# A pre-norm layer with a long convolution and a token mixer: the last inverse shuffles all on GpSimd's queue, the shortcut past them taken out, and the order of every engine written anew

## The chip, the cores and the metric

The kernel runs on one core of a Trainium2 chip. The metric is the device time of one execution in microseconds (us), lower is better. A core has five engines that run side by side, each through a queue of its own, in order: TensorE (PE; its weight loads are shown apart as PEld), VectorE (DVE), ScalarE (ACT), GpSimd (POOL) and SyncE (SP), which here only issues transfers. Transfers (DMAs) are issued by SP, POOL and once by ACT, and run on 16 DMA engines.

## The reference

```python
x = A_q                                            # 1 x 2048 x 448 (B, S, D), bf16
kv = k_shift * v          # k_shift: causal 4-tap filter of A_k along S, taps A_shift_k per channel
y  = irfft(rfft(kv, 2S) * rfft(ssm_k, 2S))[:S]     # per channel, a causal convolution of length 2048
h  = x + layernorm(x) * (y + kv * ssm_D)
u  = layernorm(layernorm(h))                       # over D
u  = gelu(einsum("bsd,sf->bdf", u, w1) + b1)       # mixes along S; F = 1792
out = h + (einsum("bdf,fs->bds", u, w2) + b2).transpose(0, 2, 1)
```

## The kernel before

The sequence index is s = 16 q + r: q is the partition (128), r a row (0 to 15) of 448 channels. The convolution is a discrete Fourier transform in two stages of matmuls, of the filter ("k", from `A_ssm_k`) and of kv ("u"), a product, and an inverse in two stages. All of SBUF is one tensor, `arena`; all of PSUM is `ps`, eight banks that are handed out to matmul groups and come free when a group is copied out (an "eviction", on ACT or DVE).

The steps, by the names that the order of work uses:

- `dummy`, `tables`, `loads`: matmuls on a constant (fillers, L1001), the sine tables E and the block matrices, and the loads. SP issues the loads of k, of the filter's four chunks of channels (L863; three of 128 rows, one of 64 rows of 4 KB) and of v.
- `kv`: transposes of k (L942), the 4-tap filter as small matmuls (L968), times v on DVE (L983).
- `kT`: transposes of the filter (L1014), eight for each half of a chunk, evicted to `KT`; behind the second half of each of the first three chunks three fillers (`N_WK`).
- `k1`, `u1` (`emit_stage1`, matmuls L1035): first stage. 16 groups each; an eviction (L1045) and, for each two groups, three shuffles (L1051) that move data to other partitions: two of 112 KB from POOL's queue, one of 224 KB from SP's. `k2`, `u2` (`emit_stage2`, L1070): second stage, evictions L715/L718 for k and L714/L717 for u, into `TK` and `TU`. One eviction covers 128 x 896.
- `i1` (`emit_products_i1`): DVE multiplies (L1136, 128 x 1792) each of 16 columns of TU with TK; for each pair of columns jj = 0 to 7, 16 matmuls (L1153), two evictions (L714, back into TU), and the inverse shuffles to `TZ` (L1176): for each of the two columns, one of 112 source rows (196 KB) on POOL's queue and one of 16 source rows (28 KB) on SP's. The small ones carry rows r = 14 and 15. In the order's names, the matmuls of jj sit in the steps i1.1, i1.4, i1.6, i1.8, i1.10, i1.12, i1.14 and i1.16; operations 9 and 18 (in i1.4 8 and 17) are the evictions, the next four the shuffles, so i1.10:19 and i1.10:21 are POOL's two.
- `ct`: transposes E into `ET` (L1084).
- `i2` (`emit_i2`): for each row r two matmuls of ET with TZ (L1275), then the gate, h, and the norms: for r below 4 an operation on DVE (L1312), for the others a gate on ACT or DVE (L1292, L1294) and L1302 on DVE; statistics on ACT, DVE and POOL; and the normalised row into `Q` (L1361, DVE).
- `mlp`: seven groups accumulate over the 16 rows of Q (L1408, seven matmuls a row, seven of the eight banks); seven more groups (L1418); then the second matrix, 16 rows of 14 matmuls (L1430), an addition on DVE (L1433) and the stores.

**The shortcut.** The last pair, jj = 7, is special before the change. Its block matrices are a permuted copy (`ML`, made on POOL in `emit_ew`), its evicted columns stay in TU, and its shuffles are four transfers of 98 KB for the rows r = 2 to 15, on SP's queue and ACT's (L1165). For r = 0 and 1 (`NZ` = 2) the data of jj = 7 are not waited for: the places are filled with zeros by two transfers, four small ones gather the needed parts of ET into `EW`, and four more matmuls for each of these two rows (L1283) add the contribution straight from TU.

**What sets the order.** `ORDER` holds, for each engine, the sequence of all its operations, found beforehand by a search. `schedule()` runs through these queues with a model of durations to hand out PSUM banks and other ring buffers; it then emits the instructions, each with the waits on semaphores that its operands need. An engine waits at the head of its queue. POOL's DMAs share eight semaphores in turn, so the ninth waits until the first has landed. The four loads of the first matrix's first half are `w1a.0` to `w1a.3` (L1381); the last three wait for the last inverse shuffles (`shuf["zl"]`).

Of the kernel before, what the change touches and what calls it, by code (L numbers as in the profile page):

```python
# [13 lines left out]
        "dummy.0:1-9 kv.4:0-11 kv.3:0-7 kv.6:0-11 kv.5:0-7 kT.1:0-7 kT.0:0-3 kT.1:9-11 kT.0:4-7 kT.3:0-7 kT.2:0-3 "  # L14
        "kT.3:9-11 kT.5:0-7 kT.2:4-7 kT.5:9-10 kT.6:0-7 kT.7:0-7 bias.0:0 kT.5:11 kv.7:0-7 k1.8:0-7 k1.9:0-7 "
        "k1.12:0-7 k1.10:0-7 kv.1:0-7 kv.2:0-11 k1.11:0-7 k1.15:0-7 k1.14:0-7 k1.13:0-7 kT.4:0-7 kv.8:0-11 "
        "kv.12:0-23 kv.9:0-27 kv.10:0-23 kv.11:0-27 k1.4:0-7 k1.0:0-1 u1.0:0-7 k1.0:2-7 u1.1:0-7 u1.2:0-7 k1.1:0-7 "
        "u1.3:0-7 kv.13:0-27 u1.4:0-7 k1.5:0-7 kv.14:0-23 k1.6:0-7 u1.6:0-7 k1.2:0-7 u1.5:0-7 kv.15:0-27 k1.7:0-7 "
        "u1.7:0-7 u1.8:0-7 u1.9:0-7 k1.3:0-7 k2.0:0-3 k2.1:0-3 k2.12:0-3 k2.13:0-3 k2.4:0-3 k2.5:0-3 kv.16:0-23 "
        "k2.9:0-3 k2.8:0-3 u1.10:0-7 u1.12:0-7 u1.13:0-7 u1.14:0-7 u1.15:0-7 u1.11:0-7 k2.2:0-3 k2.3:0-3 k2.6:0-3 "  # L20
        "k2.7:0-3 k2.10:0-3 k2.11:0-3 k2.15:0-3 k2.14:0-3 u2.0:0-3 u2.1:0-3 u2.13:0-3 u2.12:0-3 u2.8:0-2 u2.9:0-3 "
        "u2.8:3 u2.7:0-3 u2.6:0-3 i1.1:1-7 i1.1:10-16 i1.1:8 i1.1:17 i1.14:10-16 i1.14:1-7 i1.14:17 i1.14:8 "
        "i1.8:1-7 i1.8:10-17 i1.8:8 ct0.0:0-7 u2.10:0-3 u2.11:0-3 i1.10:1 i1.10:10-17 i1.10:2-8 u2.4:0-3 u2.5:0-3 "
        "i1.12:1-8 i1.12:10-17 u2.3:0-3 u2.2:0-3 i1.6:1-8 i1.6:10-17 u2.15:0-3 u2.14:0-3 i1.4:9-15 i1.4:0-7 i1.4:16 "
        "i1.16:1-7 i1.16:10-17 i1.16:8 ct.1:0-7 ct.0:0-7 ct.2:0-7 warm.0:0 i2.1:0-1 i2.2:0-3 i2.9:0-1 i2.10:0-3 "
        "i2.17:0-1 i2.45:0-1 i2.32:0-1 i2.20:0-1 i2.54:0-1 i2.28:0-1 warm.1:0 i2.41:0-1 mlp.0:1 mlp.0:4 mlp.0:2 "
        "mlp.0:0 mlp.0:6 mlp.0:3 i2.58:0-1 mlp.0:5 mlp.1:6 mlp.1:5 mlp.1:4 mlp.1:1 mlp.1:0 mlp.1:3 mlp.1:2 "
        "i2.67:0-1 mlp.2:3 mlp.2:2 mlp.2:1 mlp.2:5-6 mlp.2:4 mlp.2:0 mlp.3:4-5 mlp.3:2 mlp.3:1 mlp.3:3 mlp.3:0 "
        "mlp.3:6 i2.71:0-1 mlp.4:4 mlp.4:2 mlp.4:1 mlp.4:5 mlp.4:3 mlp.4:6 mlp.4:0 i2.80:0-1 mlp.5:1-2 mlp.5:4 "
        "mlp.5:6 mlp.5:5 mlp.5:0 mlp.5:3 i2.84:0-1 mlp.6:0 mlp.6:6 mlp.6:1 mlp.6:5 mlp.6:2 mlp.6:4 mlp.6:3 "  # L30
        "i2.93:0-1 mlp.7:6 mlp.7:0-1 mlp.7:5 mlp.7:3-4 mlp.7:2 mlp.8:2 mlp.8:6 mlp.8:5 mlp.8:3-4 mlp.8:0-1 mlp.9:3 "
        "mlp.9:1 mlp.9:6 mlp.9:0 mlp.9:5 mlp.9:4 mlp.9:2 i2.97:0-1 mlp.10:3 mlp.10:0 mlp.10:2 mlp.10:4-6 mlp.10:1 "
        "mlp.11:0 mlp.11:3 mlp.11:2 mlp.11:5 mlp.11:4 mlp.11:6 mlp.11:1 mlp.12:4 mlp.12:1 mlp.12:3 mlp.12:5 "
        "mlp.12:0 mlp.12:6 mlp.12:2 mlp.13:5 mlp.13:2 mlp.13:0 mlp.13:6 mlp.13:3 mlp.13:1 mlp.13:4 mlp.14:3 "
        "mlp.14:0 mlp.14:2 mlp.14:1 mlp.14:5 mlp.14:4 mlp.14:6 mlp.15:5 mlp.15:1 mlp.15:6 mlp.15:0 mlp.15:3 "
        "mlp.15:2 mlp.15:4 mlp.17:0-15 mlp.18:0-15 mlp.19:0-15 mlp.20:0-15 mlp.21:0-15 mlp.22:0-15 mlp.23:0-15 "
        "mlp.24:0-13 mlp.25:0-13 mlp.26:0-13 mlp.27:0-13 mlp.28:0-13 mlp.29:0-13 mlp.30:0-13 mlp.31:0-13 "
        "mlp.32:0-13 mlp.33:0-13 mlp.34:0-13 mlp.35:0-13 mlp.36:0-13 mlp.37:0-13 mlp.38:0-13 mlp.39:0-10 "
        "mlp.39:16-17 mlp.39:11 mlp.39:18-20 mlp.39:12 mlp.39:21-22 mlp.39:13 mlp.39:23-29 "
    ),  # L40
    "act": (
        "tables.0:5 kv.4:12 kv.3:8 kv.6:12 tables.6:3 tables.5:3 tables.7:5 bias.0:1 k1.8:8 k1.9:8 k1.10:8 k1.11:8 "
        "k1.13:8 k1.14:8 k1.15:8 k1.4:8 u1.0:8 u1.1:8 u1.2:8 u1.4:8 k1.5:8 k1.6:8 u1.5:8 u1.6:8 k1.7:8 u1.8:8 "
        "u1.9:8 k2.1:4 k2.13:4-5 k2.5:5 k2.9:4 u1.12:8 u1.13:8 u1.14:8 u1.15:8 k2.3:5 k2.7:5 k2.11:4 k2.15:4 u2.1:4 "
        "u2.13:5 u2.13:4 u2.9:5 u2.9:4 u2.7:4-5 i1.1:9 i1.1:18 i1.14:9 i1.14:18 i1.8:18 i1.8:9 u2.11:4-5 i1.10:18 "
        "i1.10:9 u2.5:4 i1.12:9 i1.12:18 u2.3:5 u2.3:4 i1.6:9 i1.6:18 u2.15:4-5 i1.4:8 i1.4:17 xn.1:0 xn.2:0 "
        "i1.16:18 i1.16:9 i1.16:21 ct.0:8 ct.2:8 xn.5:0 xn.4:0 ct.1:8 i2.46:0 i2.33:0 i2.19:0 i2.29:0 i2.22:0 "
        "i2.42:0 i2.31:0 i2.59:0 i2.35:0 i2.44:0 i2.68:0 i2.48:0 i2.72:0 i2.57:0 i2.81:0 i2.61:0 i2.70:0 i2.74:0 "
        "i2.94:0 i2.83:0 i2.87:0 i2.96:0 i2.100:0 mlp.16:1-2 mlp.16:6 mlp.16:4 mlp.16:0 mlp.16:3 mlp.16:5 mlp.17:16 "
        "mlp.18:16 mlp.19:16 mlp.20:16 mlp.21:16 mlp.22:16 mlp.23:16 mlp.39:15 "  # L50
    ),
    "dve": (
        "dummy.0:0 tables.3:0-1 kv.0:3 tables.6:0 tables.4:16 tables.5:0 tables.4:17 tables.6:1 tables.4:18 "
        "tables.5:1 tables.4:19 tables.6:2 tables.4:20 tables.5:2 kT.1:8 tables.7:6 kT.0:8 kT.3:8 tables.7:4 "
        "tables.7:7 kv.5:8 kT.5:8 kT.2:8 kT.7:8 kT.6:8 bias.1:0 kv.7:8 k1.12:8 kv.1:8 kv.2:12 kv.0:4 kT.4:8 kv.8:12 "
        "kv.12:24-25 kv.9:28-29 kv.10:24-25 kv.11:28-29 k1.0:8 k1.1:8 u1.3:8 kv.13:28-29 kv.14:24-25 k1.2:8 "
        "kv.15:28-29 u1.7:8 k1.3:8 k2.1:5 k2.5:4 kv.16:24-25 k2.9:5 u1.10:8 u1.11:8 k2.3:4 k2.7:4 k2.11:5 k2.15:5 "
        "u2.1:5 i1.0:0 i1.1:0 i1.14:0 i1.13:0 i1.7:0 i1.8:0 i1.9:0 i1.10:0 ct0.0:8 q.1:2 q.1:0 i1.11:0 i1.12:0 "
        "q.1:1 q.1:3 u2.5:5 i1.5:0 q.2:0 i1.6:0 i1.3:0 i1.2:0 q.2:1-2 q.3:0 i1.15:0 xn.0:1 q.2:3 i1.16:0 q.3:2 "
        "q.3:1 q.3:3 q.5:0 q.5:2 q.5:1 q.4:2 q.5:3 q.7:0 q.4:0 q.4:3 q.4:1 q.7:2 xn.3:1 q.6:0 q.6:2 q.6:1 q.6:3 "  # L60
        "i2.3:0 i2.4:0 i2.11:0 i2.5:0 i2.18:0 i2.6:0 i2.12:0 i2.21:0 i2.13:0 i2.8:0 i2.14:0 i2.55:0 i2.30:0 i2.16:0 "
        "i2.34:0 i2.43:0 i2.26:0 q.7:3 q.7:1 i2.47:0 i2.27:0 q.8:2 q.8:0 q.8:3 q.8:1 i2.39:0 i2.56:0 i2.40:0 "
        "i2.73:0 i2.60:0 i2.69:0 i2.52:0 i2.82:0 i2.85:0 i2.53:0 i2.86:0 i2.65:0 i2.66:0 i2.78:0 i2.79:0 i2.95:0 "
        "i2.98:0 i2.99:0 i2.92:0 i2.91:0 i2.105:0 i2.104:0 mlp.24:14 mlp.25:14 mlp.26:14 mlp.27:14 mlp.28:14 "
        "mlp.29:14 mlp.30:14 mlp.31:14 mlp.32:14 mlp.33:14 mlp.34:14 mlp.35:14 mlp.36:14 mlp.37:14 mlp.38:14 "
        "mlp.39:14 mlp.39:30 "
    ),
# [109 lines left out]
class _Sched:  # L177
# [145 lines left out]
    def schedule(self):  # L323
# [235 lines left out]
def _build(nc, A_q, A_k, A_v, A_shift_k, A_ssm_k, A_ssm_D, B_w1, B_b1, B_w2, B_b2, out):  # L559
# [8 lines left out]
    R = 16  # L568
# [924 lines left out]
```

## Time and profile before

| what | us |
|---|---|
| runs (median) | 174.29, 175.18, 176.02 (175.18) |
| profiled execution | 173.93 |
| its span | 172.1 |
| PE busy, share of the span | 161.4, 94% |
| DVE busy | 102.7, 60% |
| ACT busy | 90.1, 52% |
| POOL busy | 59.0, 34% |

The span runs from the first to the last instruction of the profiled execution; 1.8 us lie around it. The busy share is an average over stages with different limits: PE is dense from some 82 us to the end, ACT and DVE are dense before that. "Landing" of a transfer is when its semaphore is complete, counted from its issue.

### The profile page before, as it was taken

The numbers are of one execution on the slowest core, as the hardware profiler recorded it, in microseconds if no ns is written. First come the engines' busy times: TensorE is split into PE (matmuls) and PEld (weight loads), VectorE is DVE, ScalarE is ACT, GpSimd is POOL, SyncE is SP. The second block draws the span as 40 slices with busy tenths as digits, with TensorE's granted clock in tenths as the row PEclk, the third lists the DMA queues.
The fourth block names the chain that finished last, engine by engine and source line by source line (L and its number), as shares of the span: only waits on it lengthen the run. The fifth ranks groups of instructions, "written<-read, shape, count | busy, mean of one in ns | idle before, by whom it ended". The sixth has DMA issues, their size and how long they took to land.

```text
span 172.1 us, 3562 instructions
## 1 busy us (share of the span) xinstructions
PE 161.4 (94%) x1419; PEld 93.4 (54%) x1419; DVE 102.7 (60%) x190; ACT 90.1 (52%) x130; POOL 59.0 (34%) x152
## 2 busy tenths in 40 slices
PE   6999999979999998759999999999999999999994
PEld 2676745433333433333454555555567777777783
DVE  7998899868979999999999550000003132132231
ACT  3696757798999999989958345421210000000000
POOL 8344817690820546664898740000000000000000
PEclk9999999999999999999999999999999999999999
DMA  5999765783749677655599999993000111101111
GB/s 157 416 289 386 275 203 212 298 333 127 224 109 342 251 195 240 200 170 145 162 363 396 403 421 424 411 425 157 0 0 4 53 53 53 53 0 57 53 53 53
DMA packets 15628, 35.15 MB, mean 204 GB/s; under 512 B 3740, under 2 KB 9740, under 8 KB 15612
## 3 DMA queue, kind: packets, MB, share of 16 engines
q1 hardware_dynamic: 12468, 28.25, 45.1%
q0 software_dynamic: 2880, 6.49, 12.0%
q8 instruction: 11, 0.18, 0.4%
q10 hardware_dynamic: 264, 0.18, 0.3%
q14 instruction: 5, 0.04, 0.1%
HBM read 22.05 MB, written 1.84 MB: 139 GB/s over the span
## 4 chain that ended last, share of the span: by engine, by line
PE 63%; DMA 12%; ACT 9%; DVE 8%; issue 2%; POOL 2%; SPq 1%; DVEq 0%; POOLq 0%
PE ps L1430 24%; PE ps L1408 12%; PE ps L1418 12%; DMA arena<-arena 7%; ACT arena L714 6%; DVE arena L1136 6%; DMA arena<-in_A_ssm_k_dram 5%; PE ps L1035 4%; PE ps L1275 3%; ACT arena L1045 2%; POOL arena L1051 2%; PE ps L1070 2%; PE ps L968 2%; PE ps L1014 2%; DVE arena L983 2%
## 5 line engine op out<-in xcount | busy, mean ns | idle before, releaser
L1433 DVE SCALAR_TENSOR_TENSOR arena<-ps,arena 128x448 bf16<-128x448 f32 (+2 forms) x17 | 11.1, 656 | 56.2 <-PE ps L1430 56.2
L1430 PE MATMUL ps<-arena 128*128 128x448 bf16 (+2 forms) x238 | 42.7, 342 | 0.0
L1430 PEld LDWEIGHTS ps<-arena 128*128 128x128 bf16 x238 | 33.3, 145 | 9.5
L714 ACT CAST arena<-ps 128x896 bf16<-128x896 f32 (+1 forms) x31 | 25.0, 955 | 0.6 <-PE ps L911 0.3
L1045 ACT CAST arena<-ps 128x896 bf16<-128x896 f32 x23 | 19.5, 913 | 6.7 <-PE ps L1035 5.9
L1408 PE MATMUL ps<-arena 128*128 128x448 bf16 x112 | 22.5, 353 | 0.0
L1051 POOL DMA_DIRECT2D arena<-arena x32 | 17.5, 553 | 12.4 <-ACT arena L1045 11.8
L1418 PE MATMUL ps<-arena 128*128 128x448 bf16 x112 | 21.4, 352 | 0.0
L1398 ACT ACTIVATE arena<-ps,arena 128x448 bf16<-128x448 f32 x14 | 8.3, 637 | 18.1 <-PE ps L1418 14.4
L1136 DVE TENSOR_TENSOR arena<-arena 128x1792 bf16<-128x1792 bf16 x16 | 16.6, 1085 | 1.0 <-DMA arena<-arena 0.9
L1070 PE MATMUL ps<-arena 128*64 128x448 bf16 x128 | 15.5, 360 | 1.8 <-DMA arena<-arena 1.0
L1153 PE MATMUL ps<-arena 64*128 64x448 bf16 x128 | 14.9, 351 | 2.1 <-POOL arena L1232 0.9
L1418 PEld LDWEIGHTS ps<-arena 128*128 128x128 bf16 x112 | 11.0, 98 | 10.2
L1408 PEld LDWEIGHTS ps<-arena 128*128 128x128 bf16 x112 | 10.8, 98 | 10.6 <-DVE arena L1361 0.7
L1035 PE MATMUL ps<-arena 128*32 128x448 bf16 x256 | 15.1, 355 | 0.6 <-DVE arena L983 0.3
L1176 POOL DMA_DIRECT2D arena<-arena x14 | 8.3, 597 | 13.5 <-ACT arena L714 13.5
L1153 PEld LDWEIGHTS ps<-arena 64*128 64x128 f16 x128 | 5.9, 94 | 10.9 <-DVE arena L1136 3.7
L1070 PEld LDWEIGHTS ps<-arena 128*64 128x64 f16 x128 | 5.7, 108 | 10.7 <-ACT arena L715 2.6
L1275 PE MATMUL ps<-arena 128*128 128x448 bf16 x32 | 8.0, 353 | 2.1 <-DMA arena<-arena 1.9
L1330 ACT ACTIVATE arena<-arena 128x448 bf16<-128x448 f32 x14 | 8.0, 574 | 3.3 <-DVE arena L1302 3.1
L1035 PEld LDWEIGHTS ps<-arena 128*32 128x32 f16 x256 | 5.0, 95 | 8.4 <-DVE arena L983 2.6
L983 DVE TENSOR_TENSOR arena<-ps,arena 128x512 bf16<-128x512 f32 (+1 forms) x16 | 9.0, 617 | 0.8 <-PE ps L968 0.8
(96 smaller groups left out, 191.0 us busy)
## 6 DMA issues: line engine op xcount, KB each, us to landing
arena<-in_B_w_dram SPq DMA_DIRECT2D x8, 896.0 KB, 7.0
arena<-in_B_w_dram SPq DMA_DIRECT2D x2, 2048.0 KB, 17.0
arena<-arena SPq DMA_DIRECT2D x16, 224.0 KB, 3.4
arena<-arena POOLq DMA_DIRECT2D x32, 112.0 KB, 3.3
arena<-in_B_w_dram SPq DMA_DIRECT2D x2, 1536.0 KB, 19.1
arena<-arena POOLq DMA_DIRECT2D x14, 196.0 KB, 4.4
arena<-in_A_k_dram SPq DMA_DIRECT2D x4, 448.0 KB, 6.1
arena<-in_A_v_dram SPq DMA_DIRECT2D x4, 448.0 KB, 9.0
```

Source lines behind the costliest of these rows:

```text
L714: return e.copy(out=dst(), in_=src())
L983: return e.tensor_tensor(out=v, in0=u.rearrange("p t (r d) -> p t r d", d=64), in1=v, op=ALU.mult)
L1035: op("pe", lambda e, W, b=b, r=r, q=q, x=x, c0=c0: e.matmul(PS[32 * q:32 * q + 32, b.slots[x], 0:D], E[:, 2 * r + x, c0:c0 + 32], src[:, r ...
L1045: return e.copy(out=dst, in_=Ppair(b)) if W == "act" else e.tensor_copy(out=dst, in_=Ppair(b))
L1051: shuf[tag].append(op(q_, lambda e, W, g=g, i=i, a=a, nu=nu, jh=jh: e.dma_start(T[a + i:a + i + 4 * nu - 3:4].rearrange("p (j k) c d -> p ...
L1070: op("pe", lambda e, W, b=bs[h], h=h, j=j, c=c, par=par: e.matmul(PS[64 * par:64 * par + 64, b.slots[c], 0:D], FW[:, 64 * c:64 * c + 64], ...
L1136: op("dve", lambda e, W, m=m, i=i: e.tensor_tensor(out=MR(m.slots[0]).rearrange("p (x y) d -> p x y d", x=2), in0=TU[:, i].unsqueeze(2).br ...
L1153: k = op("pe", lambda e, W, b=bs[h], m=ms[h], par=par, t=t, tab=tab, xy=xy, P=P: e.matmul(Pb(b, par), tab[P, :], MR(m.slots[0])[P, xy, :], ...
L1275: k = op("pe", lambda e, W, b=b, r=r, h=h: e.matmul(Pb(b), ET[:, 2 * r + h, :], TZ[:, r, h, :], start=(h == 0), stop=(h == 1 and r >= NZ)) ...
L1408: op("pe", lambda e, W, r=r, fc=fc, b=bs[fc]: e.matmul(Pb(b), W1A[:, r, 128 * fc:128 * fc + 128], Q[:, r, :], start=(r == 0), stop=(r == R ...
L1418: op("pe", lambda e, W, r=r, fc=fc, b=b: e.matmul(Pb(b), W1B[:, r, 128 * (fc - n0):128 * (fc - n0) + 128], Q[:, r, :], start=(r == 0), sto ...
L1430: op("pe", lambda e, W, r=r, fc=fc, b=b, d0=d0, d1=d1: e.matmul(Pb(b)[:, d0:d1], W2[fc // 7][:, fc % 7, r:S:R], G[:, fc, d0:d1], start=(fc ...
```

## The change

1. The filter's last chunk is loaded as 128 half rows of 2 KB instead of 64 rows of 4 KB. Its 16 transposes become 32 matmuls with columns of the identity (every second one), with a result in float32; the two evictions take 128 x 512 in float32.
2. `N_WK` is 1 and only behind the first chunk: one filler for nine.
3. The shortcut is gone: `emit_ew`, EW, ML, the six small transfers on SP and the eight matmuls L1283. The last pair jj = 7 is treated like the others: for each of its two columns a shuffle of 112 rows on POOL's queue and one of 16 rows on SP's.
4. `schedule()` has other estimates (start times of the engines, two halves of the DMA engines, latencies by engine). They change which buffer is handed to which group, and no instruction.
5. `ORDER` is another for every engine. POOL's inverse shuffles went in the order jj = 6, 0, 3, 5, 4, 2, 1, while ACT evicted 0, 6, 3, 4, 5, 2, 1, 7; now they go 4, 0, 6, 3, 5, 2, 1, 7, two for each, and ACT evicts in the same order as before. SP's small ones begin with jj = 7. Two normalisations (L1245, `xn`) that ACT did ahead of the last evictions, and several of DVE's statistics (L1212, L1214), now come behind them. In PE's queue ten rows of i2, for nine, come ahead of the first mlp matmul. One u1 eviction, three of kT and one of the k transposes move from DVE to ACT, one of the k transposes and one u2 eviction from ACT to DVE; POOL issues the shuffles of u1.3 ahead of those of k1.5, as before, but the eviction k1.5 now comes before u1.2 and u1.3 on ACT. The identity is built behind the first table's three DVE operations; SP's first loads are k, filter, k, filter instead of k, k, filter, filter.

```diff
-            for i, c in enumerate((0, 1, 2, 3)):
-                op(Dq, lambda e, W, c=c: e.dma_start(KN[0:CW[c], c, :], A_ssm_k[128 * c:128 * c + CW[c], :]),
...
+            op(Dq, lambda e, W: e.dma_start(
+                KN[:, 3, 0:S // 2], A_ssm_k[384:448, :].rearrange("c (h s) -> (c h) s", h=2)),
...
+                        for h in range(2):
+                            k = op("pe", lambda e, W, b=b, rr=rr, r=8 * g + rr, h=h: e.matmul(
+                                PS[64 * h:64 * h + 64, b.slots[0], 64 * rr:64 * rr + 64], KN[:, 3, r:S // 2:R],
+                                ID[:, h:128:2], start=True, stop=True),
...
-                if i < 3:
+                if i < 1:
                     dummy(N_WK, T_KT + 1.0 * (2 * i + 1), (k,))
...
-                if jj == R // 2 - 1:
-                    for h in range(2):
-                        for par in range(2):
-                            k = op("act" if h and par == 0 else "sp", lambda e, W, j=j, h=h, p0=p0: e.dma_start(
-                                TZ[p0:p0 + 29:4, NZ:R, h, :], TU[0:8 * (R - NZ), j, h, :]),
...
-                    continue
                 for par in range(2):
...
                     for q_, a, b_, j0 in (("pool", 0, 112, 0), ("sp", 112, 128, 14)):
...
+                        if jj == R // 2 - 1:
+                            shuf.setdefault("zl", []).append(shuf["z" + q_])
...
-                            Pb(b), ET[:, 2 * r + h, :], TZ[:, r, h, :], start=(h == 0), stop=(h == 1 and r >= NZ)),
+                            Pb(b), ET[:, 2 * r + h, :], TZ[:, r, h, :], start=(h == 0), stop=(h == 1)),
...
-                    if r < NZ:
-                        for h in range(2):
-                            for jx in range(2):
-                                k = op("pe", lambda e, W, b=b, r=r, h=h, j=j, jx=jx: e.matmul(
-                                    Pb(b), EW[:, 4 * r + 2 * jx + h, :], TU[:, j, h, :], start=False, stop=(h == 1 and jx == 1)),
```

The inverse shuffles in POOL's queue, before and after (operations in between left out):

```
before: i1.14:21 i1.14:19 i1.1:19 i1.1:21 i1.8:19 i1.8:21 ... i1.12:21 i1.12:19 i1.10:21 i1.10:19 i1.6:19 i1.6:21 ... i1.4:18 i1.4:20
after:  i1.10:19 i1.10:21 i1.1:19 i1.1:21 i1.14:19 i1.14:21 i1.8:19 i1.8:21 i1.12:19 i1.12:21 ... i1.6:19 i1.6:21 i1.4:18 i1.4:20 i1.16:19 i1.16:21
```

## The prediction

> **What bounds the kernel now.** I read the chain that ended last first, backward from its end. Its columns are start, duration and what.
>
> ```profile
> 71.28 1.55 ACT arena L1245 x2
> 72.83 1.61 ACT arena L714 x2
> ...
> 75.17 3.50 DMA arena<-arena
> 78.67 0.05 issue
> 78.72 0.94 PE ps L1275 x4
> ...
> 105.95 21.19 PE ps L1418 x112
> 127.14 42.09 PE ps L1430 x231
> ```
>
> From some 82 us PE decides alone, matmul behind matmul. So the change can act only through the moment at which the mlp starts, and through PE's work from there on. I then looked at that moment in PE's timeline.
>
> ```profile
> start us, us, engine line op out<-in xcount [idle before <-releaser]
> 76.17 0.55 PE L1275 MATMUL ps<-arena 128*128 128x448 bf16 x2 [1.90 <-DMA arena<-arena]
> ...
> 81.86 1.31 PE L1408 MATMUL ps<-arena 128*128 128x448 bf16 x6
> ```
>
> The first row of i2 waits 1.90 us for a DMA. By the landings it is the last shuffle of jj = 1 on POOL's queue (76.12). It needs 5.69 us from there to the first mlp matmul (81.86): two matmuls and four of the shortcut to 77.48, then from the first L1312 (77.52) 4.34 us through DVE and POOL to a normalised row. So I next read what feeds the shuffles, ACT's and POOL's timelines, and then bandwidth by windows (the last number of a row is GB/s).
>
> ```profile
> 48.32 13.54 ACT L714 CAST arena<-ps 128x896 bf16<-128x896 f32 x16
> ...
> 48.32 23.26 ACT L714 CAST arena<-ps 128x896 bf16<-128x896 f32 x28
> ...
> 57.88 3.50 POOL L1176 DMA_DIRECT2D arena<-arena  x6 [9.60 <-ACT arena L714]
> 65.39 2.42 POOL L1176 DMA_DIRECT2D arena<-arena  x4 [1.73 <-ACT arena L714]
> 68.63 1.17 POOL L1176 DMA_DIRECT2D arena<-arena  x2 [0.82 <-ACT arena L714]
> 71.87 1.20 POOL L1176 DMA_DIRECT2D arena<-arena  x2 [1.36 <-ACT arena L714]
> ```
>
> ```profile
> 61.50:64.00 2.50, 2.50 (x27) 1.00 (x24) 2.49 (x5) 2.50 (x4) 0.96 (x2) 1.00 0.85 222
> 66.50:69.00 2.50, 2.50 (x28) 1.14 (x24) 2.50 (x5) 2.50 (x5) 1.68 (x4) 1.00 0.71 207
> 69.00:71.50 2.50, 1.53 (x15) 0.44 (x9) 2.50 (x6) 2.50 (x5) 1.51 (x4) 1.00 0.74 204
> ```
>
> POOL issues an inverse shuffle in 0.59 us, but while several are queued only 204 to 222 GB/s move, though the loads at the start reach 416. A shuffle is 112 x 1792 bytes = 200.7 kB, so the queue drains one per 0.90 to 0.98 us. The landings agree: the last eight, issued 65.39 to 72.48, land at 68.82 to 76.12, one per 1.04 us; all fourteen, pause included, one per 1.17 us. The queue of shuffles is thus nearly a bound of its own before the change, and it is kept fed from 57.88 on.
>
> **The change part by part.**
>
> *Half rows.* Chunk 3 landed 1.28 us after chunk 2, half its size; its matmuls waited 0.38 us for it. 128 rows should land in about half of that. 16 transposes took 1.18 us; 32 narrower matmuls cost between 0.033 us each (thirty of L968 in 0.99) and 0.057 (twenty of L942 in 1.14): 1.06 to 1.82 us, -0.1 to +0.6. The evictions leave DVE (2 x 0.42) for ACT (some 0.55 each, from 0.91 for 896 elements), which had 1.15 us idle there. The identity comes three DVE operations later (1.22 + 0.69 + 1.22), so the k transposes start near 5.6 instead of 4.85, covered by chunk 2, which lands at 10.50. For the first k1 matmul: -0.5 to +0.5, taken 0.
>
> *Fillers.* Eight fewer at 0.19 us are 1.5 us of PE. All but the 0.30 on the chain lay in waits for loads: 0 to -0.3, taken 0, since evictions behind it decide.
>
> *Order from 14 to 50 us.* The counts of evictions on each engine stay within one. POOL now waits for u1.3, two evictions after k1.5, and issues its two shuffles (2 x 0.54) before those of k1.5, on which k2 waits: 0 to +1.1. DVE has one u2 eviction (1.08) more ahead of the first product, against 0.94 us of idle time. I take +0.4 for the whole stage; a better order could gain up to 1.5, a worse one lose 1.5.
>
> *Product stage.* ACT has one eviction (0.83) and two normalisations (1.55) fewer ahead of the last eviction: it ends at 74.43 - 2.38 = 72.05. DVE loses two L1212, two L1214 and one small operation (1.3) before the last product; by its queue the last eviction ends near 72.2. Both say 2.2 us earlier. What moves behind is hidden under the wait for shuffles: eleven L1212 and the rest take 7.0 us from some 70.1, to 77.1; without that wait they would set the first L1312. The norms on ACT (3.0) have no reader before that either.
>
> *The shortcut's work.* On POOL 2.2 us (L1110, L1116), on SP six issues (4.35), on PE eight matmuls; all but 0.75 us (four matmuls ahead of the first L1312) lay beside other work. SP loses four issues of L1165 with ACT, and gains two small ones.
>
> *Shuffles.* POOL's queue begins with jj = 4, but ACT evicts that after 0, 6 and 3. The second eviction of jj = 4 is the sixteenth from 48.32: it ends at 61.86 by the row shown, and POOL starts 0.28 us later (the gap at 42.90 in the chain), at 62.14, instead of 57.88. The six shuffles that went out from there now stand behind it, and two more (jj = 7) follow: sixteen transfers, 3.2 MB. SP's first four small ones add 0.1 MB; the x loads are over by then. The first lands 3.0 us after its issue (the shortest of this line), and fifteen follow at 0.98 us: 62.14 + 0.4 + 3.0 + 14.7 = 80.2. Issue alone would be done at some 73.5, so the queue sets the end. Bounds: 0.90 us each and a stage 1.5 us early give 77.1; 1.17 each and 1.5 late, 84.2.
>
> *From the last landing.* All rows below 14 need it. 80.2 + 0.05 + two matmuls and their result 0.60 + 4.35 (the two first rows now alternate on DVE: 0.07 more) = 85.2. PE has meanwhile stood idle for some 6 us, more than anywhere before. Its first eight fillers started 0.37 apart, dense ones 0.19; after the idle 1.90 us nothing slowed. So 0 to 9 x 0.18 = 1.6, nearer the first as most of these matmuls are ahead of need: +0.4, 85.6. [...]
>
> From the first mlp matmul to the end the span needs 172.1 - 81.86 = 90.24, less one row of i2 that is done ahead (0.38): 89.86. Sum: 85.6 + 89.9 = 175.5, 3.4 us over the span of 172.1. The loads w1a.1 to w1a.3 start with the last landing, 1.5 us later than before, and have about 6 us until row 4 needs them.
>
> The profiled execution took 173.93, 1.25 less than the median of the runs. Laid on the median, 175.18 + 3.3 = 178.5.
>
> **The rivals.**
>
> *A, not slower: the queue drains as fast as POOL issues.* Decides below some 0.8 us a shuffle, where the last pair lands by its own issue: last eviction 72.2 + 0.28 + 0.6 + 3.64 (the pair of jj = 1, issued at 72.48) = 76.7; end 76.7 + 5.0 + 89.9 = 171.6, 0.5 less: 174.7. For it: two shuffles of a pair go to different partitions, and 414 GB/s were moved by loads. Against: the windows above, with several queued. [...]
>
> *B, faster: A, and an early stage that gains 1.5 or more* by fillers, half rows and order: 173 or less. For it: DVE and ACT are each idle for some 5 us between 14 and 50. Against: idle time there follows bank and shuffle waits, whose order changed little.
>
> *C, much slower: 1.17 us a shuffle, and a cold array*: 62.5 + 3.0 + 17.6 = 83.1, +6.9 with 1.2 for the array: 182.
>
> *D: the queue as forecast, the gain early*: the stage 1.5 us early and 0.90 us a shuffle leave the end where it was, 175.
>
> **How the numbers follow.** Forecast, as summed: 0.58; C 0.10; A 0.13; D 0.09; B 0.10. Range: 174.6 to 181.4 leaves out most of B and C. 1% (1.75 us, about what a measurement can tell from no change; the three runs lie within 0.5% of their median) divides them: faster is B and a little of A, 0.11; within 1% most of A, D and the low edge of the forecast, 0.22; slower 0.67.
>
> **What would show it.** Right: POOL's first inverse shuffles come as eight in a row after 62 us, behind a long wait for ACT; the last evictions of jj = 7 end near 72 to 73; PE then stands idle for 5 us or more until near 80, and the first mlp matmul is at 85 or later, dense from there. Wrong: PE's wait ends by 77, or the first shuffles come before 60. The half rows and fillers are right if the first k1 matmul stays within 0.5 of 13.79.

## The result, and the profile after

The changed kernel takes 181.47 us (median of 181.41 to 181.64) beside 174.74 for the kernel before in the same runs: a ratio of 1.038, interval 1.033 to 1.043. It is slower, as forecast, by 6.7 us and not by 3.3; 181.47 lies 0.07 above the range. The profiled execution has a span of 179.7 (before 172.1). Of e1, e6 and e8 below one execution each, and two of before, took over 1.5 per cent longer than the fastest of their kernel; the medians and ratios leave these out.

The chain that ended last (its longest pieces), in the lines that answer to those of before:

```profile
65.24 3.65 POOL arena L1156 x7
69.31 8.19 DMA arena<-arena
77.78 5.16 DMA arena<-arena
82.99 5.27 PE ps L1257 x17
88.29 0.70 DVE arena L1286 x2
...
92.84 1.50 PE ps L1382 x7
...
113.49 21.19 PE ps L1392 x112
134.68 42.08 PE ps L1404 x231
```

From the mlp's second seven groups on nothing changed (21.19 and 42.08 beside 21.19 and 42.09). In front of it stands what was forecast: POOL's issues, transfers, and the first rows of i2. POOL's timeline (L1156 are the inverse shuffles, before L1176):

```profile
start us, us, engine line op out<-in xcount [idle before <-releaser]
65.24 5.82 POOL L1156 DMA_DIRECT2D arena<-arena  x10 [14.80 <-ACT arena L730]
71.14 0.25 POOL L1202 TENSOR_SCALAR arena<-arena 128x2 f32<-128x2 f32 x1
71.47 1.67 POOL L1205 TENSOR_TENSOR arena<-arena 128x2 f32<-128x2 f32 x1
73.21 0.39 POOL L1214 TENSOR_TENSOR arena<-arena 128x2 f32<-128x2 f32 x1
73.80 3.00 POOL L1156 DMA_DIRECT2D arena<-arena  x5 [0.19 <-issue]
77.78 0.59 POOL L1156 DMA_DIRECT2D arena<-arena  x1 [0.99 <-DMA arena<-arena]
```

POOL waits 14.80 us, then issues ten shuffles in a row. The last issue waits for one of the eight semaphores, whose earlier transfer had yet to land: the queue of transfers, not the evictions, holds POOL there. PE's timeline (L1257 is i2, L1382 the mlp):

```profile
82.99 5.25 PE L1257 MATMUL ps<-arena 128*128 128x448 bf16 x17 [6.82 <-DMA arena<-arena]
88.73 0.55 PE L1257 MATMUL ps<-arena 128*128 128x448 bf16 x2 [0.49 <-ACT arena L1266]
...
89.50 2.85 PE L1382 MATMUL ps<-arena 128*128 128x448 bf16 x14
```

PE's wait for the last landing (82.95) grew from 1.90 to 6.82 us, and 17 matmuls of i2 then take 5.25, 0.31 each. The windows say why (the third number from the end is PE's granted clock):

```profile
79.00:81.00 2.00, 0.00 (x0) 0.00 (x0) 1.70 (x6) 1.75 (x3) 1.84 (x4) 0.75 0.86 251
83.00:85.00 2.00, 2.00 (x6) 0.87 (x7) 0.98 (x2) 0.00 (x0) 0.00 (x0) 0.50 0.45 45
86.00:87.00 1.00, 1.00 (x5) 0.46 (x4) 0.77 (x5) 0.98 (x2) 0.20 (x1) 0.59 1.05 405
```

The clock halves near 80.0 (a mean of 0.75 over 79 to 81), in the wait, and is full again near 86.8. It was at half speed once before, from 15.1 to 18.5; with that its mean over the span is 0.97, in this execution and in the three others.

Against the sum, in us:

| step | forecast | after | apart |
|---|---|---|---|
| first inverse shuffle (POOL) | 62.54 | 65.24 | +2.7 |
| from there to the last landing | 17.7 | 17.71 | 0.0 |
| to the first mlp matmul | 5.4 | 6.55 | +1.1 |
| to the end | 89.9 | 90.15 | +0.3 |

So there are two main misses: something early, and the cold array (after the wait of 6.82 us PE ran at a granted clock of 0.50). The first product (i1.0 on DVE) starts at 53.66 for 50.43, 3.2 us late, so the early stage holds the first of them.

### The profile page after: what moved, and what is told of

Its sections match the earlier page's. It is cut to its first block, busy times and chain, and to the rows that moved or that the text cites. A ratio compares the mean times of both kernels' runs of the same rounds, so it can differ in the third digit from the quotient of the medians.

```text
span 179.7 us, 3562 instructions
## 1 busy us (share of the span) xinstructions
PE 162.1 (90%) x1419; PEld 93.6 (52%) x1419; DVE 103.1 (57%) x187; ACT 92.8 (52%) x133; POOL 62.3 (35%) x150
## 4 chain that ended last, share of the span: by engine, by line
PE 63%; DMA 10%; ACT 9%; POOL 7%; DVE 6%; issue 3%; DVEq 0%; POOLq 0%
PE ps L1404 23%; PE ps L1392 12%; PE ps L1382 10%; DMA arena<-arena 10%; PE ps L1062 5%; ACT arena L1072 4%; PE ps L1257 4%; ACT arena L730 4%; PE ps L988 3%; POOL arena L1156 2%; PE ps L962 2%; DVE arena L1130 2%; POOL arena L846 2%; ACT arena L731 1%; PE ps L1040 1%
## 5 line engine op out<-in xcount | busy, mean ns | idle before, releaser
L730 ACT CAST arena<-ps 128x896 bf16<-128x896 f32 (+2 forms) x32 | 25.0, 979 | 2.3 <-PE ps L1040 2.2
L1078 POOL DMA_DIRECT2D arena<-arena x32 | 17.6, 555 | 17.5 <-ACT arena L1072 17.4
L1072 ACT CAST arena<-ps 128x896 bf16<-128x896 f32 x24 | 20.6, 909 | 5.6 <-PE ps L1062 5.5
L1382 PE MATMUL ps<-arena 128*128 128x448 bf16 x112 | 22.4, 353 | 0.1
L1392 PE MATMUL ps<-arena 128*128 128x448 bf16 x112 | 21.4, 352 | 0.0
L1062 PE MATMUL ps<-arena 128*32 128x448 bf16 x256 | 15.9, 369 | 1.0 <-DVE arena L1003 0.4
L1382 PEld LDWEIGHTS ps<-arena 128*128 128x128 bf16 x112 | 10.7, 98 | 10.9 <-DVE arena L1335 1.1
L1257 PE MATMUL ps<-arena 128*128 128x448 bf16 x32 | 9.4, 425 | 7.3 <-DMA arena<-arena 6.8
L1156 POOL DMA_DIRECT2D arena<-arena x16 | 9.4, 595 | 16.0 <-ACT arena L730 14.8
L1146 PEld LDWEIGHTS ps<-arena 64*128 64x128 f16 x128 | 5.2, 94 | 10.4 <-DVE arena L1130 5.4
```

The source lines that it names most:

```text
L730: return e.copy(out=dst(), in_=src())
L1062: op("pe", lambda e, W, b=b, r=r, q=q, x=x, c0=c0: e.matmul(PS[32 * q:32 * q + 32, b.slots[x], 0:D], E[:, 2 * r + x, c0:c0 + 32], src[:, r ...
L1072: return e.copy(out=dst, in_=Ppair(b)) if W == "act" else e.tensor_copy(out=dst, in_=Ppair(b))
L1078: shuf[tag].append(op(q_, lambda e, W, g=g, i=i, a=a, nu=nu, jh=jh: e.dma_start(T[a + i:a + i + 4 * nu - 3:4].rearrange("p (j k) c d -> p ...
L1146: k = op("pe", lambda e, W, b=bs[h], m=ms[h], par=par, t=t, tab=tab, xy=xy, P=P: e.matmul(Pb(b, par), tab[P, :], MR(m.slots[0])[P, xy, :], ...
L1156: shuf["z" + q_ + str(j)] = shuf["z" + q_] = op(q_, lambda e, W, j=j, p0=p0, a=a, b_=b_, j0=j0: e.dma_start(TZ[p0:p0 + 29:4, j0:j0 + (b_ - ...
```

## The experiments

Twelve kernels. All ratios and their intervals are to the kernel before, run beside them (medians 174.7 to 175.4); "last landing" is that of the last inverse shuffle on POOL's queue. Numbers inside a run are from its profiled execution.

### e1: POOL's shuffles in the order of the evictions

```diff
-i1.10:19 i1.10:21 i1.1:19 i1.1:21 i1.14:19 i1.14:21 i1.8:19 i1.8:21 ...
+i1.1:19 i1.1:21 i1.14:19 i1.14:21 i1.8:19 i1.8:21 i1.10:19 i1.10:21 ...
```

> The changed kernel, but GpSimd's queue begins its inverse shuffles with jj = 0, 6, 3, 4 as ScalarE evicts them, instead of 4, 0, 6, 3. Theory Q (the late start of GpSimd's queue, then 0.98 us a shuffle, sets the last landing): the first shuffle goes out near 58.8 instead of 65.2, the queue is drained before the last pair, and the last landing is set by the last pair's own issue, 75.5 + 0.3 + 0.6 + 3.6 = 80.0 instead of 82.95; 2.9 us less, some 178.6. Rival E (the queue is not the bound, the late last eviction is): unchanged, 181.5. Rival C (the cold array after the wait is the larger part): a wait of 3.8 us instead of 6.8 leaves the array warm, 4 us less or more.

Measured: 179.29, ratio 1.021 (1.016 to 1.026). Its profiled execution was its longest (181.6, half clock from 12.5 to 19.3), so I read it from the shuffles on. They start 16.8 us before the last eviction ends instead of 10.3, but they do not stay ahead:

```profile
69.33 1.17 POOL L1157 DMA_DIRECT2D arena<-arena  x2 [2.07 <-ACT arena L731]
70.56 1.58 POOL L1203 TENSOR_SCALAR arena<-arena 128x2 f32<-128x2 f32 x1
72.23 0.72 POOL L1206 TENSOR_TENSOR arena<-arena 128x2 f32<-128x2 f32 x1
73.03 0.42 POOL L1215 TENSOR_TENSOR arena<-arena 128x2 f32<-128x2 f32 x1
73.62 2.54 POOL L1157 DMA_DIRECT2D arena<-arena  x4 [0.17 <-issue]
76.65 1.17 POOL L1157 DMA_DIRECT2D arena<-arena  x2 [0.49 <-ACT arena L731]
```

Three small operations stand in front of the shuffles of jj = 2; the last six shuffles then go out close together, from 73.62 on, and land from 76.68 to 82.52, one per 1.17 us. The head of the queue is worth some 2 us, less than the 2.9 expected; a second block stands behind it, and the last landing is at 82.52 and not 80.0; e6 takes that block away.

### e2: the fillers back

```diff
-N_WZ, N_WI, N_W0, N_WK, N_WJ = 2, 0, 9, 1, 0      (behind the first chunk)
+N_WZ, N_WI, N_W0, N_WK, N_WJ = 2, 0, 9, 3, 0      (behind each of three)
```

> The changed kernel with all nine fillers back among the filter's transposes. Theory F (without fillers the array's clock falls, granted 0.50 from 15.5 to 18 us): the clock stays at 1.0, the transposes and the first k1 groups after 15 us run at full speed, the first k1 matmul moves from 17.06 to 15.9 and all behind it by 1.2 us: 180.3. Rival V (the wait of VectorE for GpSimd's table work at 9.7 to 11.0, which holds the evictions of the filter's transposes, is all of it): clock and time change little, 181.5 to 182.

Measured: 183.14, ratio 1.046 (1.040 to 1.052): dearer than after by its times (182.64 to 184.46), though the intervals of the two ratios overlap. The clock stays up behind the transposes (a granted 1.00 from 15 to 20 us, for 0.50 from 15.1 to 18.5 in after), as theory F has it, but the time is not gained. In this order PE is busy from 11 to 15 us, so the eight fillers (1.5 us) no longer lie in waits: the second half of the last chunk ends at 17.12 instead of 15.31. How much of the 1.7 us is theirs stays open, since this trace began slowly: 20 matmuls from 6 to 8 us, where after had 32 (the last section has more on it).

### e3: DVE's evictions ahead of the tables

```diff
-... tables.7:4 tables.7:6-7 kT.1:8 kT.0:8 kv.6:12 tables.3:1 kT.3:8 ...
+... kT.1:8 kT.0:8 kv.6:12 tables.3:1 kT.3:8 tables.7:4 tables.7:6-7 ...
```

> The changed kernel, but VectorE does the evictions kT.1, kT.0, kv.6 and kT.3 ahead of the three table operations that wait for GpSimd. Theory V (that wait blocks the queue and so the third chunk's transposes, 10.9 to 12.55): the third chunk's transposes start near 11.0, the first k1 matmul at 15.5 or earlier; 1.6 us less, 179.9, and if the shorter pause also keeps the clock up, 3 us less, 178.5. Theory F alone: the clock falls all the same, at most 0.5 less.

Measured: 179.73, ratio 1.024 (1.021 to 1.027), 1.7 us less than after. DVE's timeline of after shows what is taken away:

```profile
11.05 0.36 DVE L852 TENSOR_SCALAR arena<-arena 128x384 int32<-128x384 int32 x1 [1.37 <-POOL arena L850]
11.33 0.48 DVE L858 TENSOR_SCALAR arena<-arena 128x128 f32<-128x128 int32 x2
11.72 1.88 DVE L733 COPY arena<-ps 128x1024 bf16<-128x1024 bf16 x3
```

DVE stands 1.37 us before a table of POOL's, with the evictions of kT behind it, and PE waits for these from 10.86 to 12.55 with chunk 2 landed at 9.34. Moved ahead, the first k1 matmul comes at 15.95 for 17.06 (theory V: 15.5 or earlier) and the first product at 52.07 (after 53.66), in a trace that began slowly as well.

### e4: the array kept warm

```diff
-... ct.1:5-7 i2.1:0-1 ...
+... ct.1:5-7 warm.1:0 warm.2:0 ... warm.33:0 i2.1:0-1 ...
```

The `warm` matmuls (L1172, on a constant) change no result.

> The changed kernel with 34 matmuls on a constant in TensorE's queue between the last transposes of the table and the first row of i2 (32 more than it has; some 6.3 us of work, inside the wait of 6.8 us for the last shuffle). Theory C (a cold array after the wait costs the way to the first mlp matmul 1.1 us): the granted clock stays at 1.0 at 83 to 87, the first mlp matmul comes 5.4 instead of 6.5 us after the last landing, 180.3. Rival S (that way is as long because DVE, GpSimd and ScalarE pass the rows on in this order): unchanged, 181.5.

Measured: 179.53, ratio 1.024 (1.019 to 1.028), 1.9 us less than after. PE's timeline:

```profile
76.11 6.41 PE L1172 MATMUL ps<-arena 128*128 128x448 f16 x33
82.71 3.44 PE L1261 MATMUL ps<-arena 128*128 128x448 bf16 x17 [0.20 <-DMA arena<-arena]
86.87 0.74 PE L1261 MATMUL ps<-arena 128*128 128x448 bf16 x3 [0.73 <-ACT arena L1270]
87.67 2.63 PE L1386 MATMUL ps<-arena 128*128 128x448 bf16 x13
```

The same 17 matmuls take 3.44 us (the granted clock is 1.00 from 70 to 90 us), and the way from the landing (82.66) to the mlp is 5.01 instead of 6.55. The landing is 0.3 earlier, and nothing else moved: the cold array costs 1.5 us here.

### e5: the last chunk as 64 full rows again

```diff
-KN[:, 3, 0:S // 2], A_ssm_k[384:448, :].rearrange("c (h s) -> (c h) s", h=2)
+KN[0:64, 3, :], A_ssm_k[384:448, :]
-                        for h in range(2): ... e.matmul(PS[64 * h:64 * h + 64, ...], ID[:, h:128:2])
+                        ... e.transpose(out=Pbf(b, 0)[:, rr * cw:rr * cw + cw], identity=ID[0:cw, 0:cw])
```

> After, with the filter's last chunk as before: 64 rows of 4 KB, 16 transposes, evictions of 128 x 512 in bf16; the order is kept. Theory H (the 32 narrow matmuls cost 0.067 us each, 2.15 us in all, where 16 transposes take 1.18): the stretch kT.6 and kT.7 takes 1.2 us, chunk 3 lands some 0.7 later but is still not waited for, and the first k1 matmul comes 0.9 to 1.0 us earlier (17.06 to 16.1); median 180.5 +- 0.4, against 181.47 for after. Rival (the stretch is hidden: the k1 matmuls wait for the evictions on ACT or run at the same halved clock whenever they come): first k1 matmul within 0.3 of 17.06, median 181.2 to 181.8.

Measured: 180.51, ratio 1.031 (1.025 to 1.037). The stretch shrinks by 0.96 us, as theory H has it, but the first k1 matmul moves by 1.75 (17.06 to 15.31) and the first product by 2.3. The windows of after and then of e5 show the rest:

```profile
14.00:15.00 1.00, 1.00 (x20) 1.00 (x20) 1.00 (x3) 0.00 (x0) 1.00 (x4) 1.00 1.02 416
15.00:16.00 1.00, 1.00 (x14) 0.94 (x13) 0.16 (x1) 0.62 (x2) 0.26 (x4) 0.57 1.04 421
16.00:17.00 1.00, 1.00 (x11) 0.86 (x9) 0.68 (x1) 0.46 (x1) 0.00 (x0) 0.50 0.37 133
```

```profile
14.00:15.00 1.00, 1.00 (x19) 0.96 (x18) 1.00 (x3) 0.61 (x2) 1.00 (x4) 1.00 1.04 423
15.00:16.00 1.00, 1.00 (x23) 0.68 (x24) 1.00 (x3) 0.48 (x2) 0.26 (x4) 1.00 1.03 419
16.00:17.00 1.00, 1.00 (x24) 0.57 (x13) 0.99 (x2) 1.00 (x2) 0.00 (x0) 1.00 1.03 410
```

In after the clock halves at 15.1 us, as the 32 matmuls end, although PE counts as busy; in e5 it does not. Yet the time gained is only some 1 us, and the interval overlaps that of after. In e5's trace the array is cold for longer at the mlp: the clock is down from 76.5 to 86.8, and the way from the landing takes 7.60 us. In this trace the cold array took back 1.05 of the 2.3 us that the early stage gave. The other executions say the same: the mean granted clock is 0.98 in two of e5's six (179.4 and 179.5 us), 0.97 in two (180.3 and 180.7; after has 0.97 at 181.4 to 181.6) and 0.96 in two (181.5 both).

### e6: the shuffles without POOL's small operations between

```diff
-... q.1:4-5 xn.0:0 i1.6:19 i1.6:21 i1.4:18 i1.4:20 i1.16:19 i1.16:21 ...
+... i1.6:19 i1.6:21 i1.4:18 i1.4:20 i1.16:19 i1.16:21 q.1:4-5 xn.0:0 ...
```

This stands on top of e1's order.

> After, with POOL's shuffles in the order in which ACT evicts (jj = 0, 6, 3, 4, ..., as in the first experiment) and with POOL's statistics q.1:4, q.1:5 and xn.0 moved behind the shuffles of jj = 7. Theory K (in the first experiment three operations of POOL held the shuffles of jj = 2 until 73.62, and six transfers then queued up at 1.17 us each): the shuffles of jj = 2 go out by 71.2, the last landing is bound by the last eviction (some 75.5 + 0.3 + 0.6 + 3.6 = 80.0) or by the queue (first landing near 64.8 + 15 x 0.98 = 79.5): 79.5 to 80.5, first mlp matmul 1.8 to 3.0 earlier than in the first experiment; median 176.6 to 177.8. Rival (bandwidth alone decides, sixteen transfers against the other traffic): last landing still 82 or later, median 179 to 180.

Measured: 178.91, ratio 1.021 (1.013 to 1.029), no better than e1 and above theory K's 176.6 to 177.8. But the mechanism is there (the profiled execution, 180.28, is one of the longer ones):

```profile
68.48 1.17 POOL L1157 DMA_DIRECT2D arena<-arena  x2 [2.07 <-ACT arena L731]
70.91 1.17 POOL L1157 DMA_DIRECT2D arena<-arena  x2 [1.26 <-ACT arena L731]
74.15 1.17 POOL L1157 DMA_DIRECT2D arena<-arena  x2 [2.07 <-ACT arena L731]
75.81 1.17 POOL L1157 DMA_DIRECT2D arena<-arena  x2 [0.49 <-ACT arena L731]
```

Each pair goes out behind its own eviction, and the last landing is 80.81 (expected 79.5 to 80.5), 2.1 earlier than in after with the same first product (53.66). From there to the mlp it takes 7.46 us: the array is cold (a granted 0.50 until 86.4), and one more thing, which e9 and e12 show, came with this edit.

### e7: the shortcut taken out of the kernel before

```diff
-i1.16 on SP (three) and ACT (one), ew.* on POOL, ct0.1:* on SP, i2.2:0-3 and i2.10:0-3 on PE
+i1.16:19 and :21 at the end of POOL's shuffles, :20 and :22 on SP
```

> Before, with the third part of the change alone: no shortcut, the last pair jj = 7 as two shuffles at the end of POOL's queue and two small ones on SP, everything else in the order of before (POOL begins with jj = 6 at some 58). Theory Q (with the queue fed from 58 on, the last eviction sets the end): last eviction near 74.5, issues to 75.4, last landing near 79.0, first mlp matmul 84.0 to 85.0 with a partly cold array, 2.2 to 3.2 us later than in before; median 177.0 to 178.2. Rival (the shortcut alone is worth nearly all of the 6.7 us that the whole change costs): last landing 82 or later, median 180.5 or more. Second rival (the transfers drain as they are issued and the 3.0 us of saved work pay for it): last landing at 77, median 174.5 to 175.5.

Measured: 177.02, ratio 1.012 (1.006 to 1.017). The last eviction ends at 74.21, the last issue is at 75.08, the last landing at 79.05, the first mlp matmul at 84.41: as theory Q has it, each within 0.3. The third part alone costs some 2 us (1.1 to 3.0 by the interval), the colder array included: its granted clock is 0.99 or 0.98 in all four executions, and beside the executions of before at 0.99 (median 175.5) it costs 1.5. The rest of the 6.7 comes with what was changed around it.

### e8: before, with ACT's two normalisations behind the last evictions

```diff
-... xn.1:0 xn.2:0 i1.16:18 i1.16:9 i1.16:21 ...
+... i1.16:18 i1.16:9 i1.16:21 xn.1:0 xn.2:0 ...
```

> Before, with the two normalisations that ACT does ahead of the last evictions (1.55 us) moved behind them and behind the shuffle that ACT issues. The chain of before goes through these two, the evictions of jj = 7 and a shuffle into row 2 at 78.72. Theory: row 2 starts 1.0 to 1.5 us earlier, but rows 0 and 1 still wait for the landing at 76.12 and set the first mlp matmul (81.86): 0 to -0.8, median 174.4 to 175.2 beside 175.2 for before. Rival (the chain as shown decides in full): first mlp matmul at 80.5, median 173.7 or less.

Measured: 175.39, ratio 1.000 (0.996 to 1.004). In the profiled execution PE waits 2.62 us where before waited 1.90, and the clock falls 0.4 us behind the wait:

```profile
76.00:77.00 1.00, 0.43 (x3) 0.24 (x4) 0.72 (x3) 1.00 (x3) 0.54 (x2) 0.97 0.51 168
77.00:78.00 1.00, 1.00 (x4) 0.43 (x3) 0.00 (x0) 1.00 (x3) 0.92 (x2) 0.50 0.31 106
...
80.00:81.00 1.00, 1.00 (x6) 0.50 (x5) 0.32 (x2) 0.12 (x1) 0.00 (x0) 0.83 1.05 369
```

### e9: everything mended at once

The edits of e3, e5 and e6 (with e1's order), and e4's with 21 matmuls.

> After, with five things undone or mended at once: POOL's shuffles in the order of the evictions, POOL's three statistics behind them, DVE's four kT and kv evictions ahead of the tables, the filter's last chunk as 64 full rows, and 21 constant matmuls in the wait before the first row of i2 (they change no result). What stays of the change: no shortcut, one filler, the rest of the new order. Theory S (the parts add up, as each has a place of its own): early stage 2.5 to 3.2 us earlier than in after (first product 50.5 to 51.2), last landing 77.6 to 78.5, first mlp matmul 5.0 later at 82.6 to 83.5, first mlp to end 90.1, median 174.4 to 175.4, no different from before. Rival (a further loss hides in the new order, such as the granted clock or the eviction order): median 176.5 or more. Second rival (the parts overlap: half rows and DVE's wait are the same 2 us): first product at 51.4 or later, median 175.8 to 176.5.

Measured: 177.08, ratio 1.011 (1.006 to 1.016). The parts add up in the early stage (first product 49.46) and in the queue (last landing 76.58), better than theory S. But the mlp comes 7.48 us after the landing with the clock at 1.00 throughout. DVE's timeline:

```profile
70.33 0.30 DVE L1187 BATCH_NORM_AGGREGATE arena<-arena 128x2 f32<-128x6 f32 x2
73.92 0.16 DVE L1208 SCALAR_TENSOR_TENSOR arena<-arena 128x2 f32<-128x2 f32 x1 [3.30 <-POOL arena L1196]
...
78.65 1.14 DVE L1185 BATCH_NORM_STATS2 arena<-arena 128x6 f32<-128x448 bf16 x2
79.71 1.26 DVE L1277 SCALAR_TENSOR_TENSOR arena<-ps,arena 128x448 f32<-128x448 f32 x2
```

DVE stands 3.30 us before a small operation that needs the statistic I had moved behind POOL's shuffles. All its other statistics queue behind that, and row 0 (L1277) starts 3.1 us after the landing. This was my edit's doing, in e6 as well (3.30 us there too).

### e10 and e11: before with a warm array

e10 puts ten `warm` matmuls into the wait before i2.1 of the kernel before; e11 puts thirteen into e8.

> Before, with ten constant matmuls in the wait of 1.90 us before the first row of i2 (they change no result), nothing else. In the eighth experiment, whose head is that of before, the granted clock fell to 0.50 from 77 to 80 after a wait of 2.62; in the profile of before it did not fall after 1.90. Theory T (the clock falls in some executions of before too, which is why these lie between 173.8 and 176.5): the runs draw together near the lower end, median 174.0 to 174.8, spread under 1.5. Rival (before never waits long enough; the spread has another source): median 175.0 to 175.8, spread as before.

> Before, with the two normalisations on ACT behind the last evictions, as in the eighth experiment, and thirteen constant matmuls in the wait before the first row of i2 (they change no result). Theory T: the eighth experiment gained nothing since the cold array took it back (first mlp matmul 7.25 us after the last landing instead of 5.74); with a warm array that way is 5.2 to 5.7, median 173.4 to 174.6. Rival: the normalisations were never worth anything, because rows 0 and 1 wait for the landing at 76.1 in any case: as the tenth experiment, within 0.3 us.

Measured: e10 174.26, ratio 0.9954 (0.992 to 0.999), from 173.12 to 174.74; e11 174.13, ratio 0.9946 (0.992 to 0.998). Before, in the same runs, lies between 173.65 and 176.14. Both gain half a per cent, and the runs draw together toward the lower end, if not to under 1.5. In e11 the way from the landing to the mlp is 5.72, for 7.30 in e8. That the clock falls in some executions of before is not in its one trace, but in the mean granted clock of every execution: 13 of the 23 beside e10 and e11 have 0.99 (median 175.63), ten have 1.00 (174.05), and all 24 of e10 and e11 have 1.00. One fall of 3.4 us takes 0.01 off the mean (e8's trace has one, and 0.990). So the constant matmuls save that fall, and nothing else shows: e10 (174.26) is no faster than before where before stays warm. The normalisations add nothing to be measured (0.13 us between the two). e10 and e11 are the fastest versions here, half a per cent under before.

### e12: e9 without the wait on DVE

```diff
 dve: -xn.0:1 q.2:2 q.5:0 ... q.5:3      +q.2:2 q.5:0 ... q.5:3 xn.0:1
 act: -xn.2:0 ct.0:8 ct.2:8 ct.1:8       +ct.0:8 ct.2:8 ct.1:8 xn.2:0
```

> The ninth experiment, with one operation moved in two queues: DVE's small xn.0:1 behind the statistics of rows 2, 4 and 5, and ACT's xn.2 behind the three evictions of ct. In the ninth, DVE stood 3.30 us in front of xn.0:1, waiting for the statistic of POOL that had been moved behind the shuffles; the rows' statistics then held the first operation on row 0 until 79.71, 3.1 after the last landing (76.58), where the fourth experiment needed 0.6. Theory W (that wait alone is what the ninth lacked): first operation on row 0 within 1.0 of the last landing, first mlp matmul 5.0 to 5.4 after it (some 81.8), 2.0 to 2.4 earlier than in the ninth, median 174.5 to 175.2, the level of before or a little under it. Rival (the last landing slips, or the new order of i2 costs 1.5 more by itself): first mlp matmul 6.5 or more after the landing, median 176.3 or more.

Measured: 175.42, ratio 1.003 (0.999 to 1.007). The line of row 0 in DVE's timeline is now

```profile
78.73 1.28 DVE L1277 SCALAR_TENSOR_TENSOR arena<-ps,arena 128x448 f32<-128x448 f32 x2 [0.78 <-PE ps L1248]
```

0.63 us after the landing (78.10), and the first mlp matmul is at 83.11, 5.01 after it. So theory W holds for that way. The landing itself slipped by 1.5 us, with the first product at 50.91 for 49.46, so that the mlp comes 1.0 earlier than in e9 and not 2.0 to 2.4, and the median is 0.2 above the range expected.

The five mends, once the wait that one of them had made is gone, bring the changed kernel back to the time of before within the interval, still without the shortcut. One of the five, the constant matmuls, helps the old kernel too, so the loss is not gone to the last bit: beside before with a warm array (e10 at 0.9954, or the 13 of 17 executions of before beside e12 with a mean clock of 1.00, median 174.28; e12's own twelve all have 1.00) some 1.1 to 1.4 us remain. They are the shortcut's and the new order's together; no run divides them.

## Where the prediction held and where it did not

- **The queue of shuffles** (the last landing): right in place and in size, though the 0.98 to its second digit is luck: six shuffles in e1 landed one per 1.17. Fifteen landings after the first (68.24) took 14.71 us, 0.98 each, and the first landed 3.00 after its issue. Ten and not eight went out in a row, because of the late start. e6 and e7 show the other side: fed pair by pair behind the evictions, the last landing is 4.0 to 4.4 us after the last issue, and the queue is no bound. Rival A fell. Some neighbours do land close together (79.7 and 79.9 in after), but the 16 DMA engines were busy for 0.86 of the time at 215 GB/s (77 to 79 us), beside 1.02 at 414 for the loads of before at 4 us: that leaves little for a second transfer to use.
- **Half rows**: wrong. The landing came as estimated (chunk 3 0.65 us behind chunk 2, for 1.28 before). For the whole I took 0, with a bound of +0.6 for the 32 matmuls. They took 2.15 us for 1.18, 0.067 each, above both rows that I had bounded them by (0.033 and 0.057, of other shapes; the first was misread, its chain has 28 in 0.99 and 30 in 1.04, 0.035 each). And the clock that fell as they ended was in no bound. Together 2.3 us of the early stage by e5's trace, of which some 1 us is left at the end. The first k1 matmul, my test of this step, came at 17.06 for 13.79.
- **Order from 14 to 50 us**: +0.4 was the wrong place to look. The order's loss lay before 14 us, in DVE's queue, of which I had followed only the identity, and called its delay covered by chunk 2. Chunk 2 was there in time; PE waited for evictions that stood behind a table, and the table for POOL. Put ahead of it (e3): 1.7 us. I had counted which evictions changed engines, and not read what stands in front of each.
- **Fillers**: taken 0, bounds 0 to -0.3. That fewer fillers cost nothing held (e2), the size of the gain is open.
- **Product stage**: right. From the first product to the last eviction 21.85 us, for 24.00 before.
- **From the last landing**: 5.0 is exact with a warm array (5.01 in e4 and e12, at a granted 1.00). The cold array's term was mis-sized: 1.5 for +0.4, inside its bound, but near the upper end of it (1.6). My reason was that most of these matmuls are ahead of need. In DVE's queue, however, row 0's last operation (L1335) stands behind row 3's first one (L1286), which needs the 17th matmul, while POOL has row 0's scale ready at 87.35:

```profile
88.29 0.68 DVE L1286 SCALAR_TENSOR_TENSOR arena<-ps,arena 128x448 f32<-128x448 f32 x1 [0.58 <-PE ps L1257]
...
88.89 0.51 DVE L1335 TENSOR_SCALAR arena<-arena 128x448 bf16<-128x448 f32 x1
```

  An order in a queue had made matmuls urgent that row 0 does not need; this is read from the trace, and no run put row 0 first.
- **The sum of rivals**: the shortcut itself, on which the forecast was built, is worth some 2 us (e7). The rest was order, clock and half rows, which the forecast had put at +0.8 in all. That the median missed by 3.0 and the span by 4.2 most likely has this reason: the 1.25 us by which before's profiled execution lay under its median is the fall of the clock that only some executions of before have (e10), and the forecast added it to a kernel whose executions all have the same mean clock. (Rival C's sum comes to +7.1, not 6.9, which changes nothing.) Put right one at a time they give 1.7 per cent (e1), 1.4 (e3), 1.4 (e4) and 0.7 (e5, not clear of noise) of the 3.8, but they also trade with each other: behind e5's earlier landing 6.1 us of half clock were left, behind after's 3.9.

## What to carry to other kernels

Before you price a moved operation, read the queue it lands in: what stands in front of it, and who waits for it; what cost time here stood, time and again, at the head of an in-order queue (a shuffle whose eviction comes fourth, a table ahead of evictions, three statistics ahead of shuffles, row 3 ahead of row 0). Where PE waits ahead of a stretch that sets the end, count part of the stretch at half speed, and fill the wait with constant matmuls (here the granted clock was 0.50 after each of the waits of 2.62 us in e8, 4.68 in e6, 5.10 in e7, 6.82 in after and 6.85 in e5; it held after 1.90 in the trace of before, but 13 of that kernel's 23 executions beside e10 have a mean of 0.99); on the idle engine no cost of theirs showed, and they gave 1.9 us in the changed kernel and 0.8 in the old one. Look at the granted clock of every execution, not only at that of the one trace. Mend one thing at a time, and then all together, since an early gain can vanish in the clock, as 1.05 of the 2.3 us did in e5's trace.

## What the runs showed of the hardware

- **The half clock came in steps of 3.4 us, in after on one grid.** Worked out from the windows' means, the clock is at 0.50 from 76.9 to 80.3 in e8, 78.6 to 82.1 in e7, 80.0 to 86.8 in after, 79.5 to 86.4 in e6 and 76.5 to 86.8 in e5: one, one, two, two and three steps of 3.4 (the list of clock events in the trace of after has 3.41 and 6.83 us). In after the early fall (15.1 to 18.5) lies on the same grid: 15.1 + 19 x 3.41 = 79.9. The rows of e5:

```profile
76.00:77.00 1.00, 0.00 (x0) 0.00 (x0) 1.00 (x3) 1.00 (x2) 0.84 (x4) 0.77 0.92 239
83.00:85.00 2.00, 2.00 (x7) 0.88 (x6) 1.77 (x7) 1.39 (x2) 0.44 (x1) 0.50 1.00 375
86.00:87.00 1.00, 1.00 (x5) 0.28 (x4) 0.00 (x0) 0.98 (x3) 0.09 (x1) 0.61 0.96 362
```

  Work after the landing thus ran at half speed for 3.0 us in e7, 3.9 in after and 6.1 in e5, whose landing (80.71) came 0.8 behind the beginning of its second step (76.5 + 3.4). All five traces have whole steps; what sets the step no run shows.
- **A wait of 1.7 us stood ahead of the early fall.** In the early stage the clock fell in the traces of after, e1, e4 and e6, which have both the wait of 1.7 us and the 32 narrow matmuls (64 columns), and in none of e5, e9, e12 (full rows) nor e2, e3 (no such wait). In e1 it fell at 12.5, at the end of the wait and ahead of the narrow matmuls; after and e5, whose grids lie alike (86.8 in both), differ only in these. The same order does not fall every time: one of e4's four executions has a mean clock of 1.00 (the others 0.99), and so no early fall. What decides it was not tried by itself.
- **A slow start isn't shown by the clock's column.** From 6 to 8 us 20 or 21 matmuls ran in e2, e3 and e12, and 32 or more in after, e5 and e9, all at a granted 1.00 in the rows. The same 19 transposes of k took 2.04 us in e2 and e12 (from 6.16 and 6.15) and 1.24 in after (from 6.15); later seven transposes of the filter took 0.65 in all three. In after itself the column has 1.00 from 1.38 to 4.80 us, where nine fillers took 3.54, 0.39 each (33 took 6.41 in e4, 0.19 each), and the trace's list of clock events begins only with a rise to 1.00 at 4.89: the column counts what lies ahead of that as 1.00. e9 and e12 have the same order up to 70 us, and their first products are at 49.46 and 50.91. What sets the length of the slow start no run shows; these two are some 1.4 us apart, and a comparison of early stages by one trace each can be off by that much.
- **POOL's small operations had no fixed price.** The same 128 x 2 power took 0.72 us in before (L1223) and 1.67 in after (L1205, at 71.47), and the addition ahead of it 0.25 in after and 1.58 in e1. The long one in after lies beside DVE's products (two run from 71.46 on). The next power in after, at 78.72, took 0.72 with statistics on DVE and shuffles still in flight, so the shuffles alone do not do it; no run tried the products by themselves.
